# Two changes to a hand-ordered stretch: only TensorE in written order from the second batch's fourth step on, and the softmax written after the second piece of channel work

## The chip, the cores and the metric

The kernel runs on one core of one Trainium2 chip. The metric is device time in microseconds (us). The kernel before takes 1679.7 us, the median of three runs (1679.39 to 1679.97). Runs agree within about 0.3%, so a difference of a few us needs several rounds. All runs quoted here, profiled ones included, were in the fast state.

## The reference, cut to what matters

```python
# B, H, S, D = 8, 8, 576, 64; tau = 0.02
scores = matmul(q, k^T) / sqrt(D)
thresh = max(scores) - tau                  # per row
attn   = softmax(where(scores >= thresh, scores, -1e9))
x      = concat_heads(attn @ v)             # (8, 576, 512)
mixed  = real(fft(fft(x, axis=seq), axis=channel))
u      = x + mixed
un     = (u - mean(u)) / sqrt(var(u) + 1e-6)
out    = u + relu(un @ w_ch1) @ w_ch2       # w_ch1: 512x2048, w_ch2: 2048x512, given as float64
```

The weights arrive in 64 bits and the kernel turns them into 32 bits itself. That conversion is what the story turns on.

## The kernel before

The kernel walks through 8 batches of 20 steps. A step handles one row block of one pair of heads: its score products ("scores"), its softmax, the transposes of the previous step's weights ("transposed weights"), now and then a product with the values, and between these some pieces of the Fourier and channel work of earlier batches ("fill"). Steps 0 to 39 are ordered by hand: every engine's queue is in the order in which the program is written. From step 40 on only TensorE is; the other engines' queues and the transfers are ordered when the kernel is built.

```python
by_hand = ctx.enter_context(ExitStack())
by_hand.enter_context(tc.manual_schedule())            # all engines as written
...
for i in range(per_batch, 2 * per_batch):              # steps 20 to 39
    second_batch(i)
while folds:
    fold_more()
late.append(True)
by_hand.close()
ctx.enter_context(tc.manual_schedule(engines={mybir.EngineType.PE}))
for i in range(2 * per_batch, total + 1):              # steps 40 on
    ...
```

One step of the second batch (`first` counts its steps from 0):

```python
def second_batch(i):
    ...
    scores(i)
    softmax(i, None, lambda: (advance(first - 1), advance(first - 1)))
    chunks.pop(first - 1, None)
    transfers(first)
    ...
    else:                                              # first >= 3
        fill()
        transposed_weights(i - 1)
        advance(first)
        advance(first)
        fill()
        if t == 3:
            prep_pair(n + 1)
        fill()
        ...                                            # values, folds
```

`softmax` gives VectorE two reductions (L461), ScalarE two exponentials (L469), VectorE two comparisons (L477), which also free the score buffers. `advance` carries the 16 pieces of w_ch2 one stage on. A piece passes these stages, spread over two steps in the hand-written order:

```python
nc.vector.tensor_scalar(...)          # L298, int32 128x512, from the transfer's room
nc.vector.tensor_scalar(...)          # L301, int32
yield
nc.scalar.activation(...)             # L306
nc.scalar.activation(...)             # L309
nc.scalar.activation(...)             # L312
yield
nc.vector.scalar_tensor_tensor(...)   # L314, two operands
yield
nc.gpsimd.tensor_tensor(...)          # L319, multiply by the power of two
nc.gpsimd.tensor_tensor(...)          # L320, multiply by the sign
```

So there are 48 conversion instructions on VectorE and 32 on GpSimd in the second batch. Four other groups of lines come up again and again; they empty TensorE's four "mm" buffers or feed its next work: L827 and L829 (relu of the hidden layer, on ScalarE and VectorE by turns), L724 (a copy in the Fourier part whose destination is freed by GpSimd's additions L731 and L735), L562 and L564 (copies of transposed weights) and L597 (values times reciprocal sums).

Of the kernel before, what the change touches and what calls it, by code (L numbers as in the profile page):

```python
# [28 lines left out]
def _repeated(ap, n):  # L29

    return bass.AP(
        tensor=ap.tensor,
        offset=ap.offset,
        ap=[list(ap.ap[0]), list(ap.ap[1]), [0, n]],
    )
# [12 lines left out]
def kernel(  # L48
# [51 lines left out]
    by_hand = ctx.enter_context(ExitStack())  # L100
# [317 lines left out]
    def normalized(n):  # L418


        return n >= 2 * NPAIR
# [28 lines left out]
    def softmax(i, between=None, meanwhile=None):  # L450

        t = i % NT
        sc, nh = steps[i]
        neg = sb.tile([128, 2], FP32, tag="neg", bufs=3, name="neg")
        thr = sb.tile([128, 2], FP32, tag="thr", bufs=3, name="thr")
        den = sb.tile([128, 2], FP32, tag="den", bufs=3, name="den")


        e = sb.tile([128, 2 * S], FP32, tag="e", name="e")
        for j in range(nh):  # L460
            nc.vector.tensor_reduce(  # L461
                out=neg[:, j : j + 1], in_=sc[j][:, :, 0:HALF], axis=AXIS_XY, op=ALU.max,
                negate=True,
            )
        if meanwhile is not None:
            meanwhile()
        for j in range(nh):
            ej = e[:, S * j : S * (j + 1)].rearrange("p (c n) -> p c n", c=2)
            nc.scalar.activation(  # L469
                out=ej, in_=sc[j][:, :, 0:HALF], func=ACT.Exp, bias=neg[:, j : j + 1], scale=1.0  # L470
            )
            if j == 0:
                nc.scalar.activation(  # L473
                    out=thr[:, 0:nh], in_=neg[:, 0:nh], func=ACT.Identity,
                    bias=thr_off[:, :], scale=-1.0,
                )
            nc.vector.scalar_tensor_tensor(  # L477
                out=ej, in0=sc[j][:, :, 0:HALF], scalar=thr[:, j : j + 1], in1=ej,
                op0=ALU.is_ge, op1=ALU.mult, accum_out=den[:, j : j + 1],
            )  # L480

            nc.vector.tensor_scalar(
                out=den[:, j : j + 1], in0=den[:, j : j + 1], scalar1=1e-9, scalar2=None,
                op0=ALU.add,
            )
            if between is not None:
                between()
                between = None
        nc.vector.reciprocal(den[:, 0:nh], den[:, 0:nh])  # L489
        rec = None  # L490
        if normalized(i // NT):
            nc.vector.tensor_scalar(  # L492
                out=e[:, 0:S], in0=e[:, 0:S], scalar1=den[:, 0:1], scalar2=None, op0=ALU.mult
            )
            if nh == 2:
                nc.scalar.activation(  # L496
                    out=e[:, S : 2 * S], in_=e[:, S : 2 * S], func=ACT.Copy, scale=den[:, 1:2]
                )
        else:
            rec = sb.tile([128, 2 * D], FP32, tag="rec", name="rec")  # L500
            nc.gpsimd.tensor_copy(
                rec[:, :].rearrange("p (j d) -> p j d", j=nh), _repeated(den[:, 0:nh], 2 * D // nh)
            )
        if t == 4:
            nc.scalar.copy(e[:, S : S + 64], e[:, 512:S])
        steps[i] = (e, rec)

    def transposed_weights(i):
        for _ in weights_in_parts(i):
            pass  # L510
# [656 lines left out]
    per_batch = NPAIR * NT  # L1167

    def fill():
        nonlocal budget, spent  # L1170
        budget += per_slot
        if mixes:
            mix(1)
        while work and spent < budget and work[0][0] < mixed:
            done = next(work[0][1], None)
            if done is None:
                work.pop(0)
            else:
                spent += done
# [99 lines left out]
    def advance(at):  # L1279
        for run in chunks.get(at, ()):  # L1280
            next(run, None)

    def transfers(first):
        for at, j, room, issue in PLAN:
            if issue == first:
                chunks.setdefault(at, []).append(second_chunk(j, room))
# [19 lines left out]
    def mix(count):  # L1306
        nonlocal spent, mixed
        for _ in range(count):
            done = next(mixes[0], None)
            if done is None:  # L1310
                mixes.pop(0)
                mixed += 1
                break
            spent += done

    def second_batch(i):

        nonlocal budget
        n, t = divmod(i, NT)
        first = i - per_batch  # L1320
        if first != 1:
            scores(i)
        softmax(i, None, lambda: (advance(first - 1), advance(first - 1)))
        chunks.pop(first - 1, None)
        transfers(first)
        fold_more()
        if first == 0:
            transposed_weights(i - 1)
            weighted_values(n - 1, 1)
            scores(i + 1)  # L1330
            busy(4)
            folds.append(fold_rows(n - 1))
            while folds:
                fold_more()
            load_v(n + 1)
            start_batch(0)
            mix(3)
            mix(3)
        elif first == 1:
            mix(3)  # L1340
            transposed_weights(i - 1)
            busy(2)
            mix(2)
            advance(first)
            advance(first)
        elif first == 2:
            mix(2)
            transposed_weights(i - 1)
            mix(2)
            column_means(LAST)  # L1350
            copy_mean(LAST)
            mirrored(LAST)
            for c, eng in ((1, nc.vector), (3, nc.vector), (0, nc.gpsimd), (2, nc.gpsimd)):
                less_mean(eng, LAST, c)
            weighted_values(n, 0)
            advance(first)
            advance(first)
        else:
            fill()
            transposed_weights(i - 1)  # L1360
            advance(first)
            advance(first)
            fill()
            if t == 3:
                prep_pair(n + 1)
            fill()
            if t == 2:
                weighted_values(n, 0)
            if t == 0:
                weighted_values(n - 1, 1)  # L1370
                folds.append(fold_rows(n - 1))
                load_v(n + 1)
        if first == 16:
            fold_halves(1)
        if first < 3:
            budget += 3 * per_slot

    for i in range(per_batch, 2 * per_batch):
        second_batch(i)
    while folds:  # L1380
        fold_more()

    late.append(True)
    by_hand.close()
    ctx.enter_context(tc.manual_schedule(engines={mybir.EngineType.PE}))

    for i in range(2 * per_batch, total + 1):

# [82 lines left out]
```

## Time and profile before

| | us |
|---|---|
| time, median | 1679.7 |
| span of the profiled run | 1678.0 |
| TensorE idle in the span | 51.7 |
| step 20, 23, 24, 40 start at | 130.9, 170.9, 182.2, 297.1 |
| step 40 to the end | 1380.9 |

A step's start is that of its first score product. The prediction below reads the places where TensorE stands. Two of these that it left out, because they lie ahead of step 23, matter later. They are TensorE's waits between 131 and 313 us in the kernel before (total us, times, longest):

```profile
PE pv L589 <- ACT e_t L564: 6.6, 3, 3.0
...
PE pw L560 <- ACT tmp L724: 1.7, 1, 1.7
```

The first is larger than in the prediction's stretch because one of its three waits, of 3.0 us, falls in step 20; no kernel here touches it. The second, in step 22, is 1.7 us long and is about to grow.

### The profile page before, as it was taken

Reading aid. Unit: us, or ns where it says so; the run is one execution under the profiler, and the core shown is the slowest. Engines: PE = TensorE matmul, PEld = TensorE weight load, DVE = VectorE, ACT = ScalarE, POOL = GpSimd, SP = SyncE. Lnnn points to the kernel's source line nnn. Section 1 sums busy time; section 2 is a strip of 40 time slices with the busy share of each in tenths; the row PEclk is TensorE's granted clock in tenths of the full one; section 3 lists DMA queues with packets and bytes.
Section 4 is the critical chain, followed back from the end, with each engine's and each line's share of the span. In section 5 each row is a group of like instructions: output and inputs, shape, how many; then the busy total and the mean of one; then the engine's idle time right before and its main releaser. Section 6 shows DMA issues by size and latency. Waiting matters only on the chain.

```text
span 1678.0 us, 28904 instructions
## 1 busy us (share of the span) xinstructions
PE 1626.3 (97%) x10838; PEld 1277.1 (76%) x10838; DVE 1142.1 (68%) x2518; ACT 837.2 (50%) x1817; POOL 581.2 (35%) x779
## 2 busy tenths in 40 slices
PE   8998889999999999999999999999999999999998
PEld 4555555566887788878888778787878788889998
DVE  6885786565857676866576758686686858664454
ACT  5764675543545464545354546455646545432111
POOL 5773463040520433134322143213242144224232
PEclk9999999999999999999999999999999999999999
DMA  5323231010010101000101010110101010000000
GB/s 163 114 55 109 57 87 45 25 35 21 16 37 13 35 16 42 22 28 8 28 16 41 9 35 15 42 22 25 25 16 41 22 28 9 14 1 13 14 13 13
DMA packets 130384, 57.48 MB, mean 34 GB/s; under 512 B 121123, under 2 KB 121125, under 8 KB 130246
## 3 DMA queue, kind: packets, MB, share of 16 engines
q1 hardware_dynamic: 128854, 55.35, 12.3%
q8 instruction: 86, 1.41, 0.4%
q14 instruction: 52, 0.43, 0.1%
q10 hardware_dynamic: 1392, 0.30, 0.1%
HBM read 46.02 MB, written 9.44 MB: 33 GB/s over the span
## 4 chain that ended last, share of the span: by engine, by line
PE 76%; DVE 15%; ACT 7%; issue 2%; POOL 1%; DVEq 0%; ACTq 0%
PE ph L926 24%; PE po L1090 18%; PE pv L589 8%; PE sc L433 7%; PE pw L560 5%; PE po L848 3%; DVE e L477 3%; DVE neg L461 2%; ACT e L469 2%; DVE hs L1051 2%; PE sc L444 2%; PE ph L822 1%; PE py L692 1%; PE pd L112 1%; PE pa L709 1%
## 5 line engine op out<-in xcount | busy, mean ns | idle before, releaser
L469 ACT ACTIVATE e<-sc,neg 128x576 f32<-128x576 f32 x288 | 212.2, 737 | 239.5 <-DVE neg L461 238.9
L461 DVE TENSOR_REDUCE neg<-sc 128x1 f32<-128x576 f32 x288 | 206.2, 750 | 172.7 <-PE sc L433 160.9
L477 DVE SCALAR_TENSOR_TENSOR e<-sc,thr,e 128x576 f32<-128x576 f32 x288 | 229.8, 811 | 56.8 <-ACT thr L473 53.0
L1090 PE MATMUL po<-w,hs 128*128 128x256 f32 x1024 | 246.2, 383 | 0.0
L1090 PEld LDWEIGHTS po<-w,hs 128*128 128x128 f32 x1024 | 186.0, 190 | 32.8 <-issue 11.2
L926 PE MATMUL ph<-u_t,w 128*128 128x128 f32 x1536 | 187.8, 276 | 0.0
L926 PEld LDWEIGHTS ph<-u_t,w 128*128 128x128 f32 x1536 | 179.3, 192 | 4.4 <-issue 3.3
L560 PE MATMUL pw<-ident,e 128*128 128x128 f32 x1152 | 169.9, 274 | 10.5 <-ACT kT L406 2.7
L562 ACT COPY e_t<-pw 128x512 f32<-128x512 f32 x256 | 148.6, 594 | 59.9 <-PE pw L560 59.3
L433 PE MATMUL sc<-kT,qT 64*128 64x288 f32 x1024 | 167.4, 429 | 8.2 <-DVE e L477 7.6
L560 PEld LDWEIGHTS pw<-ident,e 128*128 128x128 f32 x1152 | 134.5, 141 | 29.4 <-issue 4.3
L935 DVE TENSOR_TENSOR hs<-ph,hs 128x512 f32<-128x512 f32 x160 | 107.0, 685 | 72.1 <-PE ph L926 46.8
L433 PEld LDWEIGHTS sc<-kT,qT 64*128 64x128 f32 x1024 | 92.6, 186 | 69.2 <-issue 38.8
L926 PE MATMUL ph<-t_u,s_w 128*128 128x128 f32 x1024 | 126.9, 278 | 2.1 <-POOL t_u L900 1.8
L804 DVE SCALAR_TENSOR_TENSOR u<-po,rstd,u 128x256 f32<-128x256 f32 (+1 forms) x164 | 75.5, 484 | 73.8 <-PE po L1090 71.9
L926 PEld LDWEIGHTS ph<-t_u,s_w 128*128 128x128 f32 x1024 | 120.3, 193 | 5.0 <-issue 2.3
L1090 PE MATMUL po<-hs,s_tile 128*128 128x256 f32 x512 | 122.1, 382 | 0.0
L496 ACT ACTIVATE e<-e,den 128x576 f32<-128x576 f32 x96 | 74.9, 780 | 63.6 <-DVE den L489 62.9
L1090 PEld LDWEIGHTS po<-hs,s_tile 128*128 128x128 f32 x512 | 93.6, 190 | 13.6 <-issue 2.1
L943 ACT ACTIVATE hs<-hs 128x512 f32<-128x512 f32 x112 | 69.3, 630 | 63.4 <-DVE hs L935 63.4
L622 POOL TENSOR_TENSOR half<-x 128x287 f32<-128x287 f32 x48 | 40.2, 857 | 126.5 <-ACT x L595 70.7
L492 DVE TENSOR_SCALAR e<-e,den 128x576 f32<-128x576 f32 x120 | 79.7, 664 | 3.5
(199 smaller groups left out, 2868.9 us busy)
## 6 DMA issues: line engine op xcount, KB each, us to landing
hs<-in_moe_w_ch_dram SPq DMA_DIRECT2D x23, 512.0 KB, 4.4
out_dram<-u SPq DMA_DIRECT2D x36, 256.0 KB, 2.2
qk_in<-in_q_dram SPq DMA_DIRECT2D x64, 128.0 KB, 2.4
v_in<-in_v_dram SPq DMA_DIRECT2D x64, 128.0 KB, 2.4
qk_in<-in_k_dram SPq DMA_DIRECT2D x31, 128.0 KB, 2.4
w<-in_moe_w_ch_dram SPq DMA_DIRECT2D x6, 512.0 KB, 8.3
qk_in<-in_k_dram SPq DMA_DIRECT2D x31, 64.0 KB, 2.3
stage<-in_moe_w_ch_dram SPq DMA_DIRECT2D x3, 512.0 KB, 3.9
```

The costliest lines, as they stand in the source:

```text
L433: nc.tensor.matmul(sc[j][:, c, 0:HALF], qT[hp, 128 * t : 128 * t + 128], kT[hp, HALF * c : HALF * (c + 1)], start=True, stop=True,)
L461: nc.vector.tensor_reduce(out=neg[:, j : j + 1], in_=sc[j][:, :, 0:HALF], axis=AXIS_XY, op=ALU.max, negate=True,)
L469: nc.scalar.activation(out=ej, in_=sc[j][:, :, 0:HALF], func=ACT.Exp, bias=neg[:, j : j + 1], scale=1.0)
L477: nc.vector.scalar_tensor_tensor(out=ej, in0=sc[j][:, :, 0:HALF], scalar=thr[:, j : j + 1], in1=ej, op0=ALU.is_ge, op1=ALU.mult, accum_out ...
L492: nc.vector.tensor_scalar(out=e[:, 0:S], in0=e[:, 0:S], scalar1=den[:, 0:1], scalar2=None, op0=ALU.mult)
L560: nc.tensor.transpose(pw[:, c, :], e[:, c0 : c0 + 128], ident[:, :])
L562: nc.scalar.copy(e_t[:, 4 * j : 4 * j + 4, qs], pw[:, :, :])
L589: nc.tensor.matmul(pv[64 * j : 64 * j + 64, 0:m], vt[:, 2 * c + j, :], e_t[:, 4 * j + c, 0:m] if c < 4 else ends[:, 0:m], start=(c == 0), ...
L804: nc.vector.scalar_tensor_tensor(out=u, in0=product, scalar=self.rstd[:, t : t + 1], in1=u, op0=ALU.mult, op1=ALU.add,)
L926: nc.tensor.matmul(banks[name][:, 128 * q : 128 * q + 128], left[c][:, 512 * part + 128 * q : 512 * part + 128 * q + 128], right[c], start ...
L935: nc.vector.tensor_tensor(out=to, in0=bank, in1=to if other is None else other, op=ALU.add)
L1090: nc.tensor.matmul(bank[:, 0 : DM // 2], left[p], right[p], start=start and p == 0, stop=p == NK - 1, skip_group_check=True,)
```

## The change

Its intent: the stretches after step 40 have few waits under build-time order, so let that order begin at step 23, and let the evictions and copies that TensorE waits for rank ahead of the softmax. The edit does one thing more: the last stages of a conversion (`last_stages`), which ran between the softmax's reductions and its exponentials, are now written at the start of the step. No run parts this from the late softmax.

```diff
@@ second_batch
-        softmax(i, None, lambda: (advance(first - 1), advance(first - 1)))
+        def last_stages():
+            advance(first - 1)
+            advance(first - 1)
+
+        if first < 3:
+            softmax(i, None, last_stages)
+        else:
+            last_stages()
...
             advance(first)
             advance(first)
             fill()
+            softmax(i)
             if t == 3:
                 prep_pair(n + 1)
             fill()
...
     for i in range(per_batch, 2 * per_batch):
+        if i == per_batch + 3:
+            by_hand.close()
+            ctx.enter_context(tc.manual_schedule(engines={mybir.EngineType.PE}))
         second_batch(i)
     while folds:
         fold_more()
     late.append(True)
-    by_hand.close()
-    ctx.enter_context(tc.manual_schedule(engines={mybir.EngineType.PE}))
```

## The prediction

> **What bounds the kernel now.** I read the page first, then the busy time of each engine in six stretches, then TensorE's waits in the stretch that the change touches, then the timeline of its longest wait. On the page:
>
> ```profile
> PE 1626.3 (97%) x10838; PEld 1277.1 (76%) x10838; DVE 1142.1 (68%) x2518; ACT 837.2 (50%) x1817; POOL 581.2 (35%) x779
> ```
>
> TensorE is idle for 1678.0 - 1626.3 = 51.7 us in all. No reordering of the other engines can win more than this, plus what slow clocks cost, so the first question is how much of it lies where the change acts. I placed the steps by counting the score products on TensorE in the timeline (eight records in a step, ten in each fifth). Step 20, the first of the second batch, starts at 130.9 us, step 23, where the change begins, at 170.9, step 30 at 224.4 and step 40, from where the kernel is scheduled in the new way already, at 297.1. So the changed stretch is 126 us long. The windows view:
>
> ```profile
> core 0: us, PE busy (x) PEld busy (x) DVE busy (x) ACT busy (x) POOL busy (x), PEclk, DMA share, GB/s
> 131.00:171.00 40.00, 34.09 (x186) 20.47 (x186) 22.37 (x54) 15.68 (x40) 14.36 (x19) 0.96 0.33 109
> 171.00:239.00 68.00, 59.24 (x304) 36.53 (x306) 57.36 (x120) 47.57 (x109) 38.48 (x41) 0.97 0.27 71
> 239.00:297.00 58.00, 56.15 (x314) 33.71 (x310) 38.10 (x96) 33.89 (x77) 24.06 (x36) 1.00 0.22 60
> ```
>
> The first row stays as it is. The other two are the stretch: TensorE is idle 8.8 + 1.9 = 10.6 us (of unrounded values), nearly all of it in steps 23 to 30, where VectorE is 84% busy. In no row is another engine full: TensorE stands still because of order, not of work. Who it waits for there (columns: total us, times, longest):
>
> ```profile
> PE pv L589 <- ACT e_t L564: 3.5, 2, 2.5
> PE pq L398 <- ACT hs L827: 2.1, 1, 2.1
> PE pv L589 <- POOL v_rev L536: 1.5, 1, 1.5
> PE ph L822 <- ACT hs L827: 1.2, 2, 0.9
> PE sc L433 <- DVE e L477: 0.9, 3, 0.5
> PE pw L560 <- DVE hs L829: 0.7, 1, 0.7
> PE pw L560 <- ACT u L788: 0.6, 1, 0.6
> ```
>
> All but the third and fifth are evictions that came late: a copy of transposed weights that the next product reads, or a relu or copy that frees one of the four "mm" buffers. The longest, in step 30, from the timeline (start, duration, engine, line; other rows cut):
>
> ```profile
> 229.39 0.60 PE L560 MATMUL pw<-ident,e 128*128 128x128 f32 x4
> ...
> 231.78 0.71 ACT L469 ACTIVATE e<-sc,neg 128x576 f32<-128x576 f32 x1
> ...
> 232.59 0.72 ACT L469 ACTIVATE e<-sc,neg 128x576 f32<-128x576 f32 x1
> ...
> 233.21 0.48 ACT L827 ACTIVATE hs<-ph 128x384 f32<-128x384 f32 x1
> ...
> 234.47 0.59 ACT L564 COPY e_t<-pw 128x512 f32<-128x512 f32 x1
> ...
> 235.10 3.94 PE L589 MATMUL pv<-e_t,v_rev 128*64 128x320 f32 x16 [2.53 <-ACT e_t L564]
> ```
>
> The transposes ended at 229.99, but their copy ran at 234.47: in ScalarE's queue the two exponentials of this step's softmax stood ahead of it, and ahead of those the weight conversions (L306, L309, L312). The product that waited then ran at a clock of 0.50 (windows view, 235 to 238 us) and took 3.94 us, against 2.37 for the same sixteen matmuls at 192.72.
>
> **What the Trainium skill says.** "PSUM — Partial Sum Buffer", section "Engine vs sequencer instructions": the queues of ScalarE, VectorE and GpSimdE are strict FIFO. The lines above agree: a copy whose input was ready for over 4 us ran after the exponentials. So the written order is the queue order in the manual part, and changing it is worth what such blocking costs. "TensorE: Matmul & The Clock Gate", section "What's actually happening": the array falls to half clock after an idle window of about 3.4 us. The trace shows the half clock after a gap of 2.53 us, shorter than that, so here a wait of 2.5 us already costs 3.94 - 2.37 = 1.6 us more. "SBUF — State Buffer", section "SBUF: two separate sides": VectorE and GpSimd exclude each other on a shared port pair. The trace agrees in form: the conversion instruction L301 took between 0.41 and 1.53 us, so VectorE's busy time partly contains waiting for GpSimd and can move either way.
>
> **The change, part by part.** It adds and removes no instruction. TensorE's order stays the same: the softmax has none of its instructions, and the order of scores, stretches of other work, transposes and value products is untouched. So 1626.3 us of TensorE time stand, except for the half-clock penalty. What changes is (a) that the other engines and the transfer queue are ordered at build time, by written order among what is estimated to be ready, and (b) that the softmax ranks behind two stretches of channel work and the copies of the last step's weights.
>
> Recoverable, line by line from the waits: late evictions 3.5 + 2.1 + 1.2 + 0.7 + 0.6 = 8.1 us. In each of them the input of the eviction was ready before the softmax or conversion that went first, and (b) puts it first. An eviction still has to end after its own TensorE work, so I take 80%: 6.5 us. The half clock goes with the 2.5 us wait: 1.6 us. The reversed values (L536, 1.5 us): GpSimd had been idle for 7.34 us before 201.52, when these copies could have run, so under (a) they come forward; I take two thirds: 1.0 us. Sum of the gains: 6.5 + 1.6 + 1.0 = 9.1 us.
>
> What is paid back: the scores of step i+1 need the score buffers of step i, which the last comparison of the softmax (L477) frees. From the end of the scores that chain is a reduction of 0.75, an exponential of 0.74, a small one of 0.28 and two comparisons of 0.81, about 3.4 us before hand-overs. Steps 24, 29 and 31 last 5.0 us (4.95, 4.99, 5.00), of which scores take 1.2; in step 31 the second comparison ends at 244.46 and the next scores start at 244.51. There is no room there: any eviction or conversion (0.5 to 0.7 us) put before the softmax delays the scores. VectorE confirms it: after removing the gains from steps 23 to 30, its 57.4 us would stand in about 60 us, some 95%. I let the wait of sc for L477 grow from 0.9 to 3 us: 2.1 us paid back. Conversions can slide into 239 to 297 us, where VectorE has 20 us free; the last ends at 270.35, and the first product that needs w2 starts at 278.96, so that wait stays hidden.
>
> Net 9.1 - 2.1 = 7.0 us, so 1679.7 - 7.0 = 1672.7.
>
> **The rivals.**
> 1. *The softmax chain becomes the bound* in the short steps. For: no slack in steps 24, 29 and 31, VectorE near full. Against: steps from 40 on run in this very order, and between 297 and 423 us TensorE waits only for
> ```profile
> PE pw L560 <- DVE u L804: 0.7, 1, 0.7
> PE py L692 <- ACT y_e L702: 0.3, 1, 0.3
> ```
> but those steps are 8 to 12 us long. If it holds, the gain falls to 0 to 3 us: 1677 to 1680.
> 2. *A queue blocks on a transfer.* The conversions are fed by 512 KB transfers that take 4.4 us to land, and the hand-written order leaves them a step or more. If they are placed too early, VectorE and everything behind it stands until they land; three or four such waits of 2 us undo the gain: 1679 to 1686.
> 3. *All waits go*, and the different state at step 40 also removes some of the 15 us of idle time after 297 us or its half-clock stretch at 757 us: 10.6 + 1.6 + 1.5, some 14 us: 1666. Against: the later batches settle into a repeated pattern (the same waits of 0.8 us for L562 at 955.8, 1139.7 and 1323.6), which a change before 297 us should hardly reach.
> 4. *Nothing moves*: excluded only if the order really bound TensorE, which the waits above say.
>
> **Range and chances.** Rivals 1 and 3 mark the ends, with a tail for 2: 1665.5 to 1680. Faster by over 2% would need 33.6 us, three times all the idle time of the stretch; slower by over 2% would need the build-time order to add 34 us to 126 us. So within 2% has 0.97, faster 0.01, slower 0.02.
>
> **What would show it.** In the profile after: step 40's scores near 290 instead of 297.1 us; of the waits above, L564, L827, L829 and L788 under 2 us together; pv in step 30 back at 2.4 us and no half clock near 235 us; the wait of sc for L477 grown to some 3 us; the length of the kernel after step 40 as before (1380.9 us) within 2 us. It is wrong if L477 or a transfer takes over more than 6 us, or if the part after step 40 moves by more than the part before it.

## The result, and the profile after

The changed kernel takes 1695.95 us (median of four runs, 1695.27 to 1700.70), against 1679.55 for the kernel before on the same chip. The ratio is 1.0104 with a 95% interval of 1.0085 to 1.0122. Here and below a ratio is the mean time of one kernel's fast runs over that of the other's of the same rounds, so it isn't quite the ratio of the medians. The change is within 2%, but 16.4 us slower where 7.0 us faster was expected, and outside the range of 1665.5 to 1680.

The page's first lines of the changed kernel, the busy time of each engine and the granted clock:

```profile
PE 1633.8 (96%) x10838; PEld 1281.4 (76%) x10838; DVE 1154.2 (68%) x2518; ACT 840.1 (50%) x1817; POOL 586.0 (35%) x779
...
PEclk9998799999999999999999999999999999999999
```

The instructions are the same in number. TensorE is idle 1694.5 - 1633.8 = 60.7 us, 9.0 more than before, and its own work took 7.5 us longer (1633.8 against 1626.3). The clock row says why the work is longer: slices 4 and 5, some 127 to 212 us, fell to 0.8 and 0.7. VectorE is busy 12 us longer with the same 2518 instructions.

Where the time went, by steps (differences of unrounded values):

| | before, us | after, us | difference |
|---|---|---|---|
| step 20 to step 24 | 51.3 | 70.6 | +19.2 |
| of it step 22 | 15.1 | 23.4 | +8.3 |
| of it step 23 | 11.3 | 21.8 | +10.5 |
| step 24 to step 40 | 114.9 | 111.3 | -3.6 |
| step 40 to the end | 1380.9 | 1382.1 | +1.1 |

The loss lies in two steps, and one of them, step 22, comes before the line at which the order is let go. The windows view of the kernel after (columns: stretch, its length, busy us of PE, PEld, DVE, ACT, POOL with instructions, granted clock, transfers' share, GB/s):

```profile
131.00:171.00 40.00, 28.21 (x153) 17.72 (x150) 31.38 (x69) 22.95 (x52) 19.67 (x17) 0.86 0.45 142
171.00:239.00 68.00, 54.19 (x245) 31.97 (x244) 57.18 (x89) 38.46 (x85) 47.70 (x48) 0.86 0.23 68
239.00:297.00 58.00, 57.55 (x317) 35.99 (x316) 33.15 (x90) 31.73 (x77) 13.61 (x29) 1.00 0.14 30
```

In the first row VectorE is busy 31.4 us where it was 22.4, GpSimd 19.7 where it was 14.4, and TensorE 28.2 where it was 34.1. In the last row the other engines have less to do than before, and TensorE is idle for only 0.45 us of 58. Work has moved forward in time. The VectorE part of the conversions shows how far: before step 23 starts, 26 of the 48 instructions have begun, against 3 in the kernel before.

TensorE's waits from 131 to 313 us in the kernel after:

```profile
PE pq L398 <- ACT hs L827: 9.0, 1, 9.0
PE pw L560 <- ACT tmp L724: 7.1, 1, 7.1
PE sc L433 <- DVE e L477: 3.4, 2, 1.8
PE pv L589 <- ACT e_t L564: 3.0, 1, 3.0
PE pw L560 <- DVE x_first L597: 0.7, 1, 0.7
```

The L564 wait that is left is the one of step 20. The two at the top are new in size. **Step 22.** GpSimd's timeline in the kernel after (start, duration, engine, line, operation; in brackets idle time before it and what ended it):

```profile
149.30 1.32 POOL L319 TENSOR_TENSOR w<-w,hs 128x512 f32<-128x512 f32 x1 [13.01 <-ACT y_e L702]
...
157.34 1.45 POOL L319 TENSOR_TENSOR w<-w,hs 128x512 f32<-128x512 f32 x1
158.87 1.36 POOL L320 TENSOR_TENSOR w<-w,hs 128x512 f32<-128x512 f32 x1
160.18 1.26 POOL L319 TENSOR_TENSOR w<-w,u_t 128x512 f32<-128x512 f32 x1
161.40 1.26 POOL L731 TENSOR_TENSOR u_t<-x,tmp 128x289 f32<-128x289 f32 x1
162.61 1.73 POOL L320 TENSOR_TENSOR w<-w,w 128x512 f32<-128x512 f32 x1
164.31 0.87 POOL L735 TENSOR_TENSOR u_t<-x,tmp 128x287 f32<-128x287 f32 x1
165.14 0.69 POOL L731 TENSOR_TENSOR u_t<-x,tmp 128x289 f32<-128x289 f32 x1
165.78 0.97 POOL L735 TENSOR_TENSOR u_t<-x,tmp 128x287 f32<-128x287 f32 x1
```

The four additions L731 and L735 read the tile `tmp`, and only when the last one is done may ScalarE's copy L724 write into it again. Four multiplications (L319, L320) stand between and ahead of them in GpSimd's queue, without a gap. In the kernel before the same four additions were through, 7 us earlier, before a multiplication came:

```profile
156.54 0.81 POOL L731 TENSOR_TENSOR u_t<-x,tmp 128x289 f32<-128x289 f32 x1 [3.33 <-DVE tmp L728]
...
158.98 0.80 POOL L735 TENSOR_TENSOR u_t<-x,tmp 128x287 f32<-128x287 f32 x1
160.54 1.27 POOL L319 TENSOR_TENSOR w<-w,hs 128x512 f32<-128x512 f32 x1 [0.76 <-ACT e L469]
```

What follows in the kernel after on the other engines:

```profile
166.79 0.40 ACT L724 COPY tmp<-pa 128x289 f32<-128x289 f32 x1 [4.96 <-POOL u_t L735]
...
167.24 1.12 PE L560 MATMUL pw<-ident,e 128*128 128x128 f32 x4 [7.13 <-ACT tmp L724]
```

**Step 23.** Its scores end at about 180.6 us. VectorE's timeline from then on:

```profile
178.88 2.85 DVE L314 SCALAR_TENSOR_TENSOR w<-w,w 128x512 f32<-128x512 uint32 x2
182.90 1.50 DVE L298 TENSOR_SCALAR w<-stage 128x512 int32<-128x512 int32 x1 [1.17 <-POOL w L320]
184.33 0.41 DVE L597 TENSOR_TENSOR x_first<-pv,recs 128x256 f32<-128x256 f32 x1
184.66 1.16 DVE L298 TENSOR_SCALAR w<-hs 128x512 int32<-128x512 int32 x1
185.75 1.49 DVE L301 TENSOR_SCALAR hs<-hs 128x512 int32<-128x512 int32 x1
187.15 1.49 DVE L301 TENSOR_SCALAR u_t<-stage 128x512 int32<-128x512 int32 x1
188.56 1.50 DVE L298 TENSOR_SCALAR w<-hs 128x512 int32<-128x512 int32 x1
189.99 1.75 DVE L314 SCALAR_TENSOR_TENSOR w<-hs,w 128x512 f32<-128x512 uint32 x1
191.66 1.41 DVE L461 TENSOR_REDUCE neg<-sc 128x1 f32<-128x576 f32 x2
```

The two reductions of the softmax, ready since 180.6, run at 191.66, behind the end of two L314 and six more conversion instructions that the hand-written order had elsewhere. And those are slow: 1.49 us for an L301 that elsewhere takes 0.41, 1.75 for an L314 that takes 0.68. What waits behind the reductions:

```profile
192.44 0.74 ACT L469 ACTIVATE e<-sc,neg 128x576 f32<-128x576 f32 x1 [2.48 <-DVE neg L461]
...
193.30 0.72 ACT L469 ACTIVATE e<-sc,neg 128x576 f32<-128x576 f32 x1
...
193.93 0.48 ACT L827 ACTIVATE hs<-ph 128x384 f32<-128x384 f32 x1
...
194.46 1.12 PE L398 MATMUL pq<-ident,qk_in 128*128 128x128 f32 x4 [9.01 <-ACT hs L827]
```

The exponentials stand ahead of the relu L827 in ScalarE's queue, the relu frees the buffer of the next TensorE work, so TensorE stands 9.0 us for a reduction that stood for conversions. Note what the change did not do here: this relu and the copies L548 and L562 are written ahead of the softmax of step 23, and the relu's input was there at 183.4 us, yet the build-time order put both exponentials first. From 182 to 194 us TensorE worked 2.74 us of 12, VectorE 11.10 and GpSimd 11.92; in the kernel before TensorE worked 11.69 us between the same times.

How far the shut-out goes is in the groups of two conversion lines, each with one operand form, before and then after (line, engine, operation, out<-in, times: shortest/median/longest ns, first and last start in us). Before:

```profile
L301 DVE TENSOR_SCALAR hs<-hs x7: 411/505/1531, 157.6 to 245.8; 128x512 int32<-128x512 int32 x7
...
L314 DVE SCALAR_TENSOR_TENSOR w<-hs,w x7: 675/681/703, 159.7 to 247.5; 128x512 f32<-128x512 uint32 x7
```

After:

```profile
L301 DVE TENSOR_SCALAR hs<-hs x7: 417/1462/1507, 144.7 to 212.8; 128x512 int32<-128x512 int32 x7
...
L314 DVE SCALAR_TENSOR_TENSOR w<-hs,w x7: 680/1177/1747, 148.5 to 217.4; 128x512 f32<-128x512 uint32 x7
```

The hand-written order kept L314 clear of GpSimd almost perfectly (675 to 703 ns here, and in the other nine L314 too), though not L301. In the new order they run next to each other: the median is 1.7 times as long, that of L301 nearly three times. The Trainium skill ("SBUF — State Buffer", section "SBUF: two separate sides") describes this as an exclusive lock, held for a whole instruction; an extra 1.1 us beside multiplications of about 1.3 us fits a wait of most of one instruction. A wait can be longer than that: in free_nomul, below, one L298 of 128x512 took 3.55 us, while GpSimd ended three additions (L731, L735) and ran one L377.

### The profile page after: what moved, and what is told of

Same layout as the page of the kernel before. It is cut to its first block, busy times and chain, and to the rows that moved or that the text cites. A ratio compares the mean times of both kernels' runs of the same rounds, so it can differ in the third digit from the quotient of the medians.

```text
span 1694.5 us, 28904 instructions
## 1 busy us (share of the span) xinstructions
PE 1633.8 (96%) x10838; PEld 1281.4 (76%) x10838; DVE 1154.2 (68%) x2518; ACT 840.1 (50%) x1817; POOL 586.0 (35%) x779
## 3 DMA queue, kind: packets, MB, share of 16 engines
q8 instruction: 86, 1.41, 0.4%
## 4 chain that ended last, share of the span: by engine, by line
PE 76%; DVE 14%; ACT 5%; issue 2%; POOL 2%; DMA 1%; SPq 1%; ACTq 0%; DVEq 0%; POOLq 0%
PE ph L926 23%; PE po L1090 18%; PE pv L589 8%; PE sc L433 7%; PE pw L560 6%; PE po L848 3%; PE ph L822 3%; DVE neg L461 2%; DVE e L477 2%; DVE hs L1051 2%; PE sc L444 2%; ACT e L469 2%; PE pn L782 1%; PE py L692 1%; DVE u L804 1%
## 5 line engine op out<-in xcount | busy, mean ns | idle before, releaser
L477 DVE SCALAR_TENSOR_TENSOR e<-sc,thr,e 128x576 f32<-128x576 f32 x288 | 228.9, 811 | 61.9 <-ACT thr L473 58.5
L1090 PEld LDWEIGHTS po<-w,hs 128*128 128x128 f32 x1024 | 186.0, 190 | 32.8 <-issue 11.2
L560 PE MATMUL pw<-ident,e 128*128 128x128 f32 x1152 | 170.4, 275 | 15.7 <-ACT tmp L724 7.1
L562 ACT COPY e_t<-pw 128x512 f32<-128x512 f32 x256 | 148.7, 594 | 59.9 <-PE pw L560 59.3
L560 PEld LDWEIGHTS pw<-ident,e 128*128 128x128 f32 x1152 | 134.8, 141 | 34.2 <-ACT tmp L724 7.4
```

What stands on the lines that cost most here:

```text
L477: nc.vector.scalar_tensor_tensor(out=ej, in0=sc[j][:, :, 0:HALF], scalar=thr[:, j : j + 1], in1=ej, op0=ALU.is_ge, op1=ALU.mult, accum_out ...
L560: nc.tensor.transpose(pw[:, c, :], e[:, c0 : c0 + 128], ident[:, :])
L562: nc.scalar.copy(e_t[:, 4 * j : 4 * j + 4, qs], pw[:, :, :])
L1090: nc.tensor.matmul(bank[:, 0 : DM // 2], left[p], right[p], start=start and p == 0, stop=p == NK - 1, skip_group_check=True,)
```

## The experiments

There were 17 runs. The texts on record name theories by letters: A is that the freed order costs, because it pulls conversions forward; B that the late softmax costs; the letters that come later are variants, put forward when an earlier one had missed. In each diff `...` marks cuts. The base is the kernel before for free_only, late_only, before_nomul and weights_first, the changed kernel for pinned, late_from_7 and after_nomul, the run named just before for pinned_pool, seam_early and weights_first_23, and free_only for the rest.

### First set: which half of the change, and do the conversions carry it?

The kernel before had a median of 1679.53 us in these rounds.

**free_only**: the order is let go at step 23; the softmax stays in its early place.

```diff
+        if i == per_batch + 3:
+            by_hand.close()
+            ctx.enter_context(tc.manual_schedule(engines={mybir.EngineType.PE}))
```

> Half of the change: from step 23 on only TensorE keeps the written order, but the softmax stays written ahead of the channel work, as before. Theory A (the freed order lets weight conversions, L298 to L320, run ahead of the hand-ordered work of steps 21 to 23, and TensorE waits for that work): 1690 to 1700 us, with waits of over 5 us in steps 22 and 23 as in the changed kernel. Theory B (the late place of the softmax is what costs): at most 1682 us, no wait over 3 us in steps 22 and 23.

Measured: 1690.68 us, ratio 1.0065 (1.0050 to 1.0080). 24 of the 48 conversion instructions precede step 23, and the two waits are there (TensorE's waits of this kernel from 131 to 340 us):

```profile
PE pq L398 <- ACT hs L827: 7.9, 1, 7.9
PE pw L560 <- ACT tmp L724: 7.1, 1, 7.1
```

So letting the order go is worth 11.2 us of the 16.4, and its loss lies in the same two steps. Steps 24 to 40 take 107.0 us, 7.9 fewer than before: the waits that the prediction wanted to remove do go, without the late softmax. That gain isn't all due to order, since most conversions are over when the stretch begins.

**late_only**: the other half; the hand order holds to step 40 as in the kernel before, and the softmax goes behind the second fill.

```diff
+        if first < 3:
+            softmax(i, None, last_stages)
+        else:
+            last_stages()
...
             fill()
+            softmax(i)
```

> The other half: all engines keep the written order through the second batch, but the softmax is written behind the second stretch. Theory A: no conversion runs ahead, so no wait over 5 us in steps 22 and 23, and late evictions (L827, L564) are shortened: 1670 to 1682 us. Theory B: over 1688 us, with TensorE waiting for L477 or for the transposed weights of late softmaxes.

Measured: 1719.69 us, ratio 1.0242 (1.0227 to 1.0257), 40 us slower; A's 1670 to 1682 missed, B held. TensorE waits for L477 at the start of most steps from 24 on, 29.6 us in all. One of these waits, behind the softmax of step 36, where no conversion runs any more (the timeline of this kernel):

```profile
313.23 0.56 DVE L829 TENSOR_SCALAR hs<-ph 128x384 f32<-128x384 f32 x1 [3.39 <-PE ph L822]
...
313.71 1.41 DVE L461 TENSOR_REDUCE neg<-sc 128x1 f32<-128x576 f32 x2
...
315.94 0.82 DVE L477 SCALAR_TENSOR_TENSOR e<-sc,thr,e 128x576 f32<-128x576 f32 x1 [0.82 <-ACT thr L473]
...
316.91 0.72 PE L433 MATMUL sc<-kT,qT 64*128 64x288 f32 x2 [2.63 <-DVE e L477]
```

VectorE stood 3.39 us for a relu that TensorE had not got to, with the reductions, long ready, behind it in the queue. The step took 8.3 us in place of 5.0. This is the prediction's first rival, in a program where the written order is the queue's order. In the changed kernel the L477 waits are 3.4 us in all, so there the order at build time spares most of this.

**pinned**: the changed kernel, with each conversion stage held behind the last instruction that the previous step has on VectorE, ScalarE and GpSimd.

```diff
 def advance(at):
     for run in chunks.get(at, ()):
-        next(run, None)
+        with ExitStack() as behind:
+            for one in anchors:              # last one of the step before, per engine
+                behind.enter_context(tc.issue_after(one))
+            next(run, None)
```

> The changed kernel, but each stage of a conversion written in step i (23 and later) must stand, on its own engine, behind the last instruction written there before step i; everything else is free as in the change. Theory A: the waits of 7.1 us (L724) and 9.0 us (L827) and the half clocks near 163, 187 and 211 us go, the gains of steps 25 to 36 stay: 1668 to 1678 us. Theory B: the conversions are not the cause, over 1690 us.

Measured: 1705.36 us, ratio 1.0159 (1.0142 to 1.0176), slower than the change itself. Steps 22 and 23 were mended: 3 conversion instructions before step 23, as by hand, and step 24 at 183.6 us. But then waits for L477 add up to 14.8 us in steps 25 to 35. So the early conversions are indeed what broke steps 22 and 23, and theory A's time (1668 to 1678) missed because the loss came back elsewhere.

**pinned_pool**: the same, with GpSimd's two multiplications alone held.

```diff
-            for one in anchors:              # VectorE, ScalarE, GpSimd
+            for one in anchors:              # GpSimd only
```

> As the last, but only GpSimd's two multiplications of a conversion (L319, L320) are held behind the work of the step before; VectorE's and ScalarE's parts are still free to run ahead. Theory A with the queue length alone as the cause: the wait for L724 in step 22 goes (GpSimd's queue is clear), the one for L827 in step 23 stays over 5 us, 1684 to 1692 us. Theory C (the cost of step 23 is mostly VectorE and GpSimd shutting each other out, the conversions on VectorE taking 1.5 us in place of 0.4): both waits fall under 3 us and VectorE's L301 goes back to a mean under 0.8 us: 1672 to 1684 us.

Measured: 1688.51 us, ratio 1.0054 (1.0039 to 1.0069). The L724 wait of 7.1 us is gone, L301 has a mean of 636 ns (828 in the kernel before, 1057 in the changed one), and step 24 starts at 184.5 us. So 7.4 of the change's 16.4 us go with the place of the multiplications. Theory C's signs came true, but the time stays above its 1672 to 1684. In both held kernels one score product of step 23 slipped ahead of part of step 22's transposes on TensorE, so TensorE's order isn't strictly the same; the later held kernels tie that place.

### Second set: is there a place for the conversions at which letting go pays?

The kernel before: 1679.53 us again. From here on the softmax is early unless said.

**pinned_early**: the order let go, conversions held on three engines at every step, the seam on TensorE tied.

```diff
+        if first >= 3:
+            anchor()                          # VectorE, ScalarE, GpSimd
+        if first == 3:
+            with tc.issue_after(last_on_TensorE):
+                scores(i)
```

> Order freed from step 23 as in the change, softmax in its early place, and every conversion stage of step i held behind the last instruction that its engine was given before step i. Theory A (bunched conversions are what freeing costs; 24 or more of their 48 VectorE instructions ran before step 23 in place of 3): steps 22 and 23 last under 17 and 13 us again, no wait over 3 us there, and step 24 starts by 185 us: 1668 to 1680 us. Theory D (freeing the order costs by itself, the build-time order being worse than the hand's for the softmax and the evictions too): over 1685 us.

Measured: 1688.47 us, ratio 1.0050 (1.0035 to 1.0065). Step 24 starts at 184.5 us, and then L477 costs 8.2 us in four waits. Letting the order go costs 9 us even with the conversions held in their steps (theory D). Of the profile's loss 2.8 us lie in steps 20 and 23 and 6.3 between steps 24 and 40; some of the 2.8 is a matter of half clocks, as free_from_14 shows below.

**seam_early**: held only once, behind the end of step 22.

```diff
-        if first >= 3:
+        if first == 3:
             anchor()
```

> As the last, but the conversions are held only behind the last instruction written before step 23; from there on they are free. It parts two forms of theory A. A1 (the harm is that they run ahead of the hand-ordered steps 21 and 22): step 22 is mended, step 23 too, 1668 to 1680 us. A2 (the harm is that they come in a bunch, wherever it lies): step 22 is mended, but a wait of over 5 us for L827 or L477 stands in step 23 or 24: 1684 to 1692 us.

Measured: 1689.13 us, ratio 1.0056 (1.0041 to 1.0071). Steps 22 and 23 are mended; the crowd and its waits move to steps 27 and 28 (L788 with 4.0 us, L562 with 3.4, L597 with 2.1). The time is A2's, but the wait came later and was smaller than A2 said.

**free_from_7**: the order let go at step 27.

```diff
-        if i == per_batch + 3:
+        if i == per_batch + 7:
```

> Softmax early, the order freed from step 27 in place of 23, when eight of the sixteen conversions are done and the rooms of the others are not free yet. Theory A: nothing to bunch before step 26, so steps 22 and 23 as before (step 24 starts near 182 us), and the waits of 2.5, 0.9 and 1.0 us of steps 30, 32 and 35 shrink: 1668 to 1678 us. Theory D: over 1682 us.

Measured: 1687.30 us, ratio 1.0045 (1.0028 to 1.0062). Theory A missed, D held. Steps to 25 are as before; steps 26 to 29 lose 7.8 us, the first of them ahead of the release again. VectorE's conversions stand 5.4 us for transfers and 2.9 us for GpSimd's L320; in the kernel before they stood for neither.

**late_from_7**: the whole change, from step 27.

```diff
-        if first < 3:
+        if first < 7:
             softmax(i, None, last_stages)
...
-        if i == per_batch + 3:
+        if i == per_batch + 7:
```

> The whole change (order freed and softmax late), but from step 27 on. Theory A: bunching is avoided as in the run before, and what the late place costs by itself shows as the difference to it: 3 to 6 us as between the changed kernel and the one with the order freed alone, so 1672 to 1684 us. If the late place costs only where conversions are bunched, the two agree within 2 us.

Measured: 1694.05 us, ratio 1.0083 (1.0068 to 1.0098). The late place costs 6.75 us on top of free_from_7: L829 makes TensorE stand 4.1 us in step 27, and L477 does for 10.1 us where it was 2.2. That is over the 3 to 6 us expected.

### Third set: is it the multiplications, and does the written place matter?

The kernel before: 1680.52 us.

**before_nomul** and **free_nomul**: the kernel before and free_only without L319 and L320 for w_ch2. Both give a wrong result on purpose.

```diff
     yield
+    if unscaled:                              # set from step 20 on
+        return
     nc.gpsimd.tensor_tensor(...)              # L319
     nc.gpsimd.tensor_tensor(...)              # L320
```

> Wrong on purpose, a control for the next run: the kernel before without GpSimd's two multiplications (L319, L320) of the w2 conversions, 16 times 2.7 us of GpSimd. By the trace of before it should win little, the wait for v_rev (1.5 us) and some of VectorE's stretched instructions: 1673 to 1680 us.

Measured: 1675.11 us, ratio 0.9969 (0.9956 to 0.9983).

> Wrong on purpose: order freed from step 23, softmax early, without the same multiplications. Theory C (the cost of freeing comes by way of GpSimd: its queue filled with conversions, and VectorE shut out while it works): at most 2 us above the control, VectorE's L298, L301 and L314 at means near 0.42, 0.42 and 0.68 us, no wait over 3 us in steps 22 and 23. Theory D (the build-time order of conversions among softmax and evictions is worse by itself): 6 us or more above the control.

Measured: 1676.08 us, ratio 0.9976 (0.9962 to 0.9989). Letting the order go costs 1.0 us between these two, with intervals that overlap, against 11.2 between the whole kernels. Theory C's time came true, two of its signs did not: a wait over 3 us stays in step 23, and L298, L301 and L314 have means of 0.64, 0.54 and 0.77 us. The conversions run as far ahead as before, 24 of the 48 before step 23, and now the same place is cheap. TensorE's waits of free_nomul from 131 to 313 us (its line numbers are four higher here than elsewhere: L398, L560, L827 and L724 are L402, L564, L831 and L728):

```profile
PE pq L402 <- ACT hs L831: 3.9, 1, 3.9
...
PE pw L564 <- ACT tmp L728: 1.7, 1, 1.7
```

The wait of step 22 is back at 1.7 us, the kernel before's. The one of step 23 is halved but not gone, because conversions still stand ahead of the reductions, most of them at their normal length (one took the 3.55 us named above). Step 23 takes 16.9 us, 5.6 more than in before_nomul, and steps 24 to 40 give it back. So the place alone costs what later steps repay, and the cost comes with GpSimd's multiplications. The runs don't split it between their place in GpSimd's queue, their shutting out of VectorE, and the late release of the transfers' rooms (VectorE stood 3.6 us for transfers in free_only, 0 in free_nomul): all three leave with them.

**conv_last**: free_only with the conversions written at the very end of each step.

```diff
-        softmax(i, None, last_stages)
-        chunks.pop(first - 1, None)
-        transfers(first)
+        softmax(i)
...
-            advance(first)
-            advance(first)
             fill()
...
+        last_stages()                         # at the end of the step, from 23 on
+        chunks.pop(first - 1, None)
+        transfers(first)
+        advance(first)
+        advance(first)
```

> Order freed from step 23, softmax early, all conversion stages and transfers of a step written at its end, behind its softmax, evictions and value products, so that they rank last. Theory E (they go first because they were written first): 1670 to 1682 us, few conversions before step 23. Theory F (they are put where the build-time estimate sees an engine idle, whatever their rank, and the estimate is too short): 1685 us or more, 20 or more of VectorE's 48 conversion instructions still before step 23.

Measured: 1689.31 us, ratio 1.0052 (1.0038 to 1.0065). The waits of 7.1 and 7.9 us are the same, and 26 of the 48 precede step 23. Within a step the written rank of a conversion doesn't decide its place under the build-time order. That the place comes from an estimate of when things are ready is the natural reading; the runs show only that rank isn't it.

**free_from_11**: the order let go at step 31 (five rounds).

```diff
-        if i == per_batch + 3:
+        if i == per_batch + 11:
```

> Softmax early, order freed from step 31, when three of sixteen conversions are left, of which two need the same room one after the other. If the cost of freeing is the conversions, nothing is left to bunch: steps to 30 as before, the waits of 0.9 us (step 32) and 1.0 us (step 35) go: 1676 to 1679.5 us, at or a little below the kernel before. Theory D: 1682 us or more.

Measured: 1684.91 us, ratio 1.0024 (1.0010 to 1.0037), missing the 1676 to 1679.5. With few conversions left, one was put ahead of its transfer. In the timeline of this kernel:

```profile
242.90 0.94 DVE L298 TENSOR_SCALAR w<-hs 128x512 int32<-128x512 int32 x1 [2.13 <-DMA hs<-in_moe_w_ch_dram]
...
245.14 0.48 DVE L597 TENSOR_TENSOR x<-pv,recs 128x320 f32<-128x320 f32 x1
...
245.68 2.85 PE L822 MATMUL ph<-u_t,w 128*128 128x384 f32 x8 [1.20 <-DVE x L597]
```

VectorE stood 2.13 us for 512 KB to land, the eviction L597 stood behind it, and TensorE behind that. Steps 30 and 31 together took 23.1 us where they had taken 20.1 (two score products of step 31 slipped ahead of step 30's value products, so the two can't be told apart); waits for L477 of 1.9 and 1.5 us came with it. Here the prediction's second rival is seen at work. Another 2.4 us of this profile's loss lie in steps 20 and 23, ordered by hand as before; free_from_14, below, takes this up.

### Fourth set: what was still open

The prediction was wrong and no held version had mended it. Still open: whether the multiplications alone, held, would save the freed order with an early softmax; what the late softmax costs without them; and whether a release after nearly all conversions is free. The kernel before: 1678.77 us.

**pinned_pool_early**: free_only with only the multiplications held, the seam tied.

```diff
+        if first >= 3:
+            anchor()                          # GpSimd only
```

> Order freed from step 23, softmax early; only GpSimd's two multiplications of a conversion are held behind GpSimd's work of the step before, while VectorE's and ScalarE's parts may still run ahead. C1 (the harm is GpSimd's queue standing in front of the last spectral sums, L731 and L735, in step 22, and VectorE slowed while conversions and multiplications bunch there): 1678 to 1684 us, and the 7.1 us wait of step 22 is gone. C2 (GpSimd's 43 us of multiplications shut VectorE out wherever they lie when the order is freed): 1686 to 1690 us, as with all three engines held.

Measured: 1694.11 us, ratio 1.0091 (1.0077 to 1.0105). It missed C1, and was worse than C2 allowed. Step 22 is mended, as C1 said. What VectorE waited for between 171 and 313 us in this kernel has three lines that the kernel before has not at all:

```profile
DVE w L298 <- DMA hs<-in_moe_w_ch_dram: 8.9, 2, 5.5
...
DVE w L298 <- DMA stage<-in_moe_w_ch_dram: 4.9, 1, 4.9
...
DVE w L298 <- DMA w<-in_moe_w_ch_dram: 3.4, 2, 2.9
```

That is 17.2 us. A transfer's room comes free only when the multiplication L320 has read the sign out of it; held multiplications free it late, the transfer starts late, and the next conversion, already placed early in VectorE's queue, blocks everything behind it.

**after_nomul**: the changed kernel without the multiplications; wrong on purpose.

```diff
     yield
+    if unscaled:
+        return
     nc.gpsimd.tensor_tensor(...)
```

> Wrong on purpose: the changed kernel without the same multiplications. It shows what the late place of the softmax costs where GpSimd is out of the way. If the late place costs by itself: 4 to 8 us above the freed order without multiplications (1676), 1680 to 1684 us, with waits for L477 in steps 24 to 27. If it only costs together with the bunching on GpSimd: within 2 us of it.

Measured: 1678.15 us, ratio 0.9999 (0.9985 to 1.0012). Against free_nomul the late softmax costs 2.1 us by the medians or 3.9 by the ratios, from different rounds with intervals that just overlap: small, if it is there, and between the two forecasts. In the whole kernel it was 5.3 us (16.4 - 11.2).

**free_from_14**: the order let go at step 34 (five rounds).

```diff
-        if i == per_batch + 3:
+        if i == per_batch + 14:
```

> Softmax early, order freed only from step 34, when one conversion's last stages are left. Nothing can be bunched; the wait of 1.0 us for L564 in step 35 may go: 1677.5 to 1680 us, at or just below the kernel before. Over 1683 us would mean that freeing the order costs even without conversions.

Measured: 1682.74 us, ratio 1.0025 (1.0011 to 1.0039), missing the 1677.5 to 1680. Of its profile's loss 1.3 us lie in step 35, after the release. Much of the rest is half clock where the order had not changed: 1.0 us in step 20, 1.3 in step 23 (from 178.7 us on) and 1.6 in step 62 (at 537 us); the kernel before's stretch at 757 us, absent here, gives 1.2 back. A wait of 0.8 us in step 73, which before_nomul and weights_first have too, costs 1.0.

The record shows why step 23 differs. In each of the 19 traces half-clock stretches begin whole multiples of 3.413 us apart, and this grid lies differently against the steps from trace to trace. All six kernels that have step 23 by hand as before have its wait of 2.1 us for L827. In before, free_from_7, late_from_7 and weights_first a grid line parts it: TensorE is busy at least 59% of each cell, and the clock stays. In free_from_11 and free_from_14 it falls into one cell with TensorE busy for 38%, and the next cell runs at half clock. So losses of 1 to 3 us in one profile can be the grid's; what places the grid isn't on record.

### Fifth set: is there a faster version by hand?

If late evictions were worth 8 us, then mending some of them by hand should show it. The kernel before: 1679.63 us; both have five rounds.

**weights_first**: all by hand; in steps 25, 30 and 35 the copies of transposed weights are written ahead of the softmax.

```diff
+        if first >= 3 and t == 0:
+            transposed_weights(i - 1)
         softmax(i, None, lambda: (advance(first - 1), advance(first - 1)))
...
-            transposed_weights(i - 1)
+            if t != 0:
+                transposed_weights(i - 1)
```

> A version by hand, all engines in written order through the second batch as before: only in the first step of each pair (steps 25, 30 and 35) the transposes of the last step's weights and their copies are written ahead of the softmax and of the channel work. If the blocked copies (L564) are what the waits of 2.5 us with its half clock (1.6 us) in step 30, 1.0 us in step 35 and 0.3 us in step 25 come from, most of 5.4 us goes: 1673 to 1677 us. If another wait takes their place (the softmax is written later by the copies' 1.5 us, and the next scores wait for it): 1678 to 1681 us.

Measured: 1679.83 us, ratio 0.9997 (0.9983 to 1.0011). The L564 waits of 2.5 and 1.0 us and the half clock at 235 us are gone. In their place, in TensorE's waits of this kernel from 171 to 297 us:

```profile
PE pe L544 <- POOL rec L501: 2.2, 1, 2.2
...
PE pw L560 <- ACT u L788: 1.6, 1, 1.6
```

The first is new, the second was 0.6 us, and a half clock at 201.0 us is new too. At step 40 this kernel was 1.7 us ahead in its profile; a half-clock stretch at 532 us cost 1.6 of that.

**weights_first_23**: the same, with the first fill of step 23 ahead of its softmax too.

```diff
+        if first == 3:
+            fill()
         softmax(...)
...
-            fill()
+            if first != 3:
+                fill()
```

> As the last, and in step 23 alone the first stretch of channel work is written ahead of the softmax, so that its relu (L827) frees its buffer before the exponentials: the wait of 2.1 us there falls to under 1 us: 1 to 2 us below the run before; or the softmax of step 23 comes late and gives it back: the same within 0.7 us.

Measured: 1679.40 us, ratio 0.9999 (0.9986 to 1.0011). The L827 wait shrank from 2.1 to 0.7 us, and a wait for the copies L548 of 1.1 us took its place: the same as the run before within 0.7 us. No version that computes the right result beat the kernel before.

## Why the prediction was wrong, point by point

**What bounds the kernel**: right. TensorE's order and work stood, and every loss found here is TensorE standing or running at a lower clock.

**"1626.3 us of TensorE time stand, except for the half-clock penalty"**: right in form. The exception was sized at a gain of 1.6 us; TensorE's work became 7.5 us longer instead, at a granted clock of 0.86 in both stretches; half clocks began at 163.0 and 186.9 us, within the two new waits, and at 210.8.

**The recoverable waits**: they did go, but not by the step named. Both L564 waits of its stretch went, and v_rev (L536) and L788 too; from 239 to 297 us TensorE stood 0.45 us. But "(b) puts it first" was said to do it, and free_only does nearly the same without (b). Nor does (b) put it first: in step 23 the exponentials ran ahead of L827, L548 and L562, all written before them, and that wait grew from 2.1 to 9.0 us. (One reading was loose as well: in the kernel before, the L829 of 0.7 us stood behind the channel work's statistics L790, and not directly behind a softmax or conversion.) By hand, weights_first removed L564 and nothing was measured in time, as two other waits rose: here a sum of waits, even at 80%, overstated what removing them was worth.

**The softmax chain, paid back with "0.9 to 3 us"**: right in size, 3.4 us. The late place as a whole was mis-sized: it cost about 5.3 us in the changed kernel and 40 by hand.

**The failed step** is part (a), "the other engines and the transfer queue are ordered at build time", which the sum booked only as a gain of 1.0 us for L536. The prediction left the cost of conversions that come early to a rival. With it fell "Conversions can slide into 239 to 297 us", as they went the other way, and "The first row stays as it is", as 26 of 48 instead of 3 came before step 23, and step 22, ahead of the release, lost 8.3 us. In the sum's terms the runs showed +11.2 us for (a) (free_only). Without GpSimd's multiplications it is 1.0 (free_nomul against before_nomul), not told apart from nothing.

**The rivals**: the first, the softmax chain, is what late_only and the pinned kernel ran into. The second, "A queue blocks on a transfer", named the right family, a conversion placed too early with everything behind it in a strict queue. In the changed kernel VectorE stood only 4.5 us for its conversions' transfers and GpSimd; the missing half was that early conversions are also long, beside GpSimd's multiplications, and that GpSimd's own queue blocks L724. In pinned_pool_early and free_from_11 the rival was met as written. The third put the idle time after 297 us at 15 us; the trace has 17.5 between TensorE's instructions there.

**Its own tests**: step 40 was to start near 290 us and started at 312.4. L564, L827, L829 and L788 were to be under 2 us together in steps 23 to 39 and were 9.5. The part after step 40 was to stay within 2 us, and did. The product in step 30 takes 2.37 us again, as forecast. The condition named for failure, L477 or a transfer above 6 us, did not occur: the cause came from a third place.

**What could have been read beforehand**: the prediction itself noted that L301 took between 0.41 and 1.53 us and concluded that VectorE's time "can move either way". All sixteen L314 at 675 to 703 ns were a sign that the hand-written order kept this one clear of GpSimd, so that for L314 losing it could only go one way.

**What stays open**: how the 11.2 us divide between GpSimd's queue, the shut-out of VectorE and the rooms that come free late; what places the grid of the half clocks; and why the build-time order chooses the places it does.

## What to carry to other kernels

Before you hand a stretch to an order chosen at build time, list the work in it that has no deadline of its own, here the conversions, and ask where it lands if it goes as early as its inputs allow, also ahead of the line where the hand order ends. Look for instructions whose durations are tightly packed next to a relative that varies threefold: here that was the only place where the hand order's keeping VectorE and GpSimd apart showed. And test each half of a change by itself; here one half cost 11.2 us, the other about 5 beside it and 40 alone.

## What the Trainium skill lacked or had wrong

- "SBUF — State Buffer", section "SBUF: two separate sides", gives the lock between VectorE and GpSimd but no durations for these operations. Here, beside GpSimd multiplications of 1.3 to 1.7 us on 128x512, VectorE's int32 `tensor_scalar` grew from 0.41 to 1.50 us and its two-operand `scalar_tensor_tensor` from 0.68 to 1.75 us. The page also leaves out what follows for order: in a strict queue the loss is passed on to whatever stands behind, here a 1.41 us pair of reductions that was 11 us late.
- "TensorE: Matmul & The Clock Gate", section "What's actually happening", has the half clock come after an idle window of about 3.4 us. In the kernel before it came after a gap of 2.53 us in step 30, in a stretch of 3.41 us of which TensorE worked 1.08 us. The section calls the window free-running, and the traces agree (the grid of 3.413 us above); what it lacks is the cost of one half-clock stretch within a kernel, here about 1.0 to 1.6 us a stretch, enough to cover a lead of 1.7 us as in weights_first.
- No page says what a build-time order costs compared with a hand-written one. Here it put conversions ahead of transfers that had not landed, so that VectorE stood 17.2 us in one kernel (pinned_pool_early) where by hand it stood 0, and moved work to before the step at which the hand order ended (step 22 grew by 8.3 us).
